# Moving an attention kernel's sums to VectorE, half of its k copies to ScalarE and its transposes later

## Chip, cores, metric

One core of a Trainium2 chip. The metric is device time in microseconds (us) of one execution; lower is better. Profiles are of one execution each; their spans are some 2 us shorter than the timed figure of the same execution. Runs of one kernel scatter: the kernel before took 337.5 to 350.8 us within one set of rounds. So comparisons rest on several runs of each kernel, taken in the same rounds on the same chip, and a run over 1.5% above the fastest of its kernel counts as slow and is left out.

## The reference, cut to what matters

```python
# q, k, v: (8 batches, 8 heads, 576 positions, 64), fp32
q_d, k_d, v_d = means of q, k, v over groups of 4 positions
out = repeat(softmax(q_d k_d^T / 8) v_d, 4)            # coarse attention
    + softmax(q k^T / 8 where |i - j| < 4) v           # local band attention
x = out as (4608 tokens, 512)
y = gelu(x @ w_in) @ w_out                             # w_in 512 x 2048, w_out 2048 x 512
```

The kernel computes in fp16 with fp32 sums. x is processed in 9 chunks of 512 tokens. **M1** is x @ w_in with the gelu (64 matmuls of 128x512 a chunk), **M2** is g @ w_out (64 more). The attention of batch b is woven into M2 of chunk b-1.

## The kernel before

```python
def m1(c):                       # a generator: each yield is one matmul
    ...
    for j in range(3 if c == 0 else 0, NJ):
        ps = mm()                # two PSUM tiles in turn
        for fc in range(4):
            nc.tensor.matmul(out=ps, lhsT=w_in_sb[:, fc, 128*j:128*j+128],
                             rhs=xT[:, fc, 512*c:512*c+512], start=(fc == 0), stop=(fc == 3))
            if fc == 3:
                nc.scalar.activation(out=g[:, j, :], in_=ps, func=ACTF.Gelu)
            yield

def cross_k():                   # regroup on VectorE, then turn by a DMA transpose
    for i in range(NP): regroup("kn", i)
    nc.sync.dma_start_transpose(out=kP..., in_=REG["kn"])
def cross_q(b): ...              # the same for q

def k_in(p):                     # k as the score matmuls want it, and its sums of four
    for hh in range(2):
        nc.vector.tensor_copy(out=kz[r, p, hh, :].rearrange("p (t r) -> p t r", r=6),
                              in_=kP[r, :, p, :].rearrange("p r t -> p t r"))
    ...                          # three VectorE adds
def q_sums(b, p): ...            # two adds on GpSimd
def v_down(b): ...               # five small operations on GpSimd

# chunk c, b = c + 1 (for 1 < b < 7; batch 7 is the last and loads no next one)
load6(b+1, "kn"); load6(b+1, "qn")
v_down(b)
for p in range(NP): k_in(p); q_sums(b, p)
k_lo()
run(load_v(b+1)); cross_k()
f1()                             # all of M1
attn(b, f2)                      # attention; f2(n) drops n matmuls of M2 between its parts
```

In `attn`, a pair p of heads goes through `scores` (matmuls, then exponentials on ScalarE), `mask` (VectorE times the band), `av` (matmuls, then the norm on VectorE) and `t_out` (transposes, then an add into xT). `cross_q(b + 1)` stood behind the first mask. A PSUM tile is a buffer that matmuls write their sums to; with two in turn, M1's next matmuls wait until ScalarE's gelu has read the older one. Names in the profile lines: `k_turned` and `qT` are k and q after their transposes, `kz` is k laid out for the score matmuls, `kdz` and `KL` hold k's sums of four, `q_t` and `qd` q's, `v_d` and `v_lm` v's; `sc` are scores, `e` exponentials, `sl` the scores against `KL`.

The softmax here doesn't subtract the row's maximum and nothing guards it: scores larger than these inputs give would overflow.

## Time and profile before

| | before |
|---|---|
| timed, us (first 3 runs) | 348.05 median, 344.29 to 350.76 |
| profiled span, us | 340.5 (of another execution, timed at 342.2) |
| TensorE busy | 325.6 us, 96% |
| stages of chunks 1 to 6, us (start of M1 to start of the next M1) | 37.8, 36.6, 35.2, 35.2, 34.4, 34.3 |

The stages come from the starts of the M1 blocks in the TensorE timeline. The prediction below shows the lines behind them. Beside those, the timeline of the queue that issues the transposes tells when each begins (start, length of the issue, line):

```profile
62.02 3.94 SPq L143 DMA_TRANSPOSE k_turned<-k_nat  x1
66.09 10.72 SPq L148 DMA_TRANSPOSE qT<-q_nat  x1
88.80 8.48 SPq L143 DMA_TRANSPOSE k_turned<-k_nat  x1
97.39 8.61 SPq L148 DMA_TRANSPOSE qT<-q_nat  x1
120.29 5.99 SPq L143 DMA_TRANSPOSE k_turned<-k_nat  x1
126.44 7.43 SPq L148 DMA_TRANSPOSE qT<-q_nat  x1
```

M1 of chunk 1 begins at 67.8 and needs the second batch's k and q some 15 us later; M1 of chunk 2 begins at 105.6. From batch 4 on (the third k and q above), q's transpose is issued 13 to 16 us ahead of the M1 of its stage.

### The profile page before, as it was taken

How to read it: one execution, taken by the hardware profiler on the slowest of the kernel's cores; microseconds unless marked ns; L12 is line 12 of the kernel's file. 1: busy time of each engine (PE TensorE's matmuls, PEld its weight loads, DVE VectorE, ACT ScalarE, POOL GpSimd, SP SyncE). 2: the span in 40 equal slices, each digit the busy share in tenths (PEclk: the TensorE clock that was granted, in tenths of full speed). 3: DMA queues.
4: the chain of work that ended last, by engine and by line, in shares of the span. 5: the costliest groups of instructions: out<-in, count | busy, mean ns of one | idle time of the engine just before them, and what ended most of it. 6: DMA issues, size and time to landing. Idle time of an engine off the chain costs nothing.

```text
span 340.5 us, 6382 instructions
## 1 busy us (share of the span) xinstructions
PE 325.6 (96%) x2586; PEld 178.6 (52%) x2586; DVE 210.4 (62%) x388; ACT 200.5 (59%) x368; POOL 145.9 (43%) x182
## 2 busy tenths in 40 slices
PE   7999999899799997999999999999999999999995
PEld 4665555544464455545654565446544654444444
DVE  7955945839977968695869686878695650000000
ACT  9675875467464675467646754675467646524610
POOL 8973393344961687393807780085560000000000
PEclk9999999999999999999999999999999999999999
DMA  6999999996699999989991999909950010011011
GB/s 80 166 193 204 202 171 201 163 167 75 68 128 156 194 121 172 185 128 164 154 129 58 128 119 178 126 3 130 192 88 0 33 64 31 2 62 63 0 54 71
DMA packets 99693, 39.34 MB, mean 116 GB/s; under 512 B 71632, under 2 KB 95184, under 8 KB 99664
## 3 DMA queue, kind: packets, MB, share of 16 engines
q0 software_dynamic: 66304, 22.42, 64.2%
q1 hardware_dynamic: 28320, 7.34, 22.3%
q10 hardware_dynamic: 5040, 9.18, 9.7%
q8 instruction: 20, 0.33, 0.4%
q14 instruction: 9, 0.07, 0.1%
HBM read 44.83 MB, written 9.44 MB: 159 GB/s over the span
## 4 chain that ended last, share of the span: by engine, by line
PE 75%; DVE 14%; DMA 6%; ACT 3%; issue 1%; POOL 1%; DVEq 0%
PE m_ps L233 32%; PE m_ps L257 28%; DMA k_turned<-k_nat 4%; PE sc L383 3%; DVE e L421 3%; DVE nall L458 3%; PE av L443 2%; DMA k_nat<-in_k_dram 2%; DVE kz L269 2%; PE tr_o L485 2%; DVE q_nat L135 2%; DVE k_nat L135 1%; PE m_ps L248 1%; DVE kdz L278 1%; PE av L435 1%
## 5 line engine op out<-in xcount | busy, mean ns | idle before, releaser
L257 PE MATMUL m_ps<-w_out_sb,gT 128*128 128x512 f16 x560 | 130.5, 379 | 0.0
L233 PE MATMUL m_ps<-xT,w_in_sb 128*128 128x512 f16 x564 | 125.5, 379 | 0.8 <-DVE xT L488 0.5
L236 ACT ACTIVATE gT<-m_ps 128x512 f16<-128x512 f32 x141 | 84.2, 597 | 38.8 <-PE m_ps L233 37.2
L233 PEld LDWEIGHTS <-w_in_sb 128*128 128x128 f16 x564 | 54.6, 98 | 66.4 <-issue 3.0
L257 PEld LDWEIGHTS <-gT 128*128 128x128 f16 x560 | 51.9, 98 | 54.3
L289 POOL TENSOR_TENSOR q_t<-qT 128x288 f32<-128x288 f16 x28 | 25.2, 898 | 63.1 <-DMA qT<-q_nat 62.9
L261 ACT COPY out_sb<-m_ps 128x512 f32<-128x512 f32 x35 | 20.6, 589 | 45.2 <-PE m_ps L257 45.2
L269 DVE COPY kz<-k_turned 64x576 f16<-64x576 f16 x48 | 36.2, 754 | 6.8 <-DMA k_turned<-k_nat 6.1
L421 DVE TENSOR_TENSOR e<-e,band 128x1152 f16<-128x1152 f16 x28 | 27.5, 981 | 20.6 <-ACT e L415 20.6
L488 DVE TENSOR_TENSOR xT<-tr_o,xd 128x576 f16<-128x576 f16 x28 | 21.2, 756 | 23.1 <-ACT xd L487 23.1
L252 DVE COPY out_sa<-m_ps 128x256 f32<-128x256 f32 x2 | 0.8, 424 | 55.1 <-PE m_ps L248 55.1
L458 DVE TENSOR_TENSOR nall<-av,rr 128x896 f16<-128x896 f32 x30 | 32.7, 1092 | 1.0
L113 POOL DMA_DIRECT2D v_win<-in_v_dram x30 | 27.0, 922 | 0.5 <-PE sc L383 0.5
L383 PE MATMUL sc<-qT,kz 128*128 128x114 f16 (+2 forms) x320 | 25.6, 216 | 0.0
L487 ACT COPY xd<-tr_o 128x144 f16<-128x144 f16 x28 | 7.7, 274 | 27.6 <-PE tr_o L485 24.8
L413 ACT ACTIVATE e<-sc 128x684 f16<-128x684 f32 x32 | 23.5, 736 | 0.0
L383 PEld LDWEIGHTS <-kz 128*128 128x128 f16 x320 | 21.5, 97 | 1.4
L278 DVE TENSOR_TENSOR kdz<-k_t 64x144 f16<-64x144 f32 x48 | 18.6, 387 | 1.4
L415 ACT ACTIVATE e<-sc 128x468 f16<-128x468 f32 x32 | 18.1, 566 | 0.7 <-PE sc L383 0.7
L443 PE MATMUL av<-v_win,e 128*128 128x65 f16 x300 | 14.1, 194 | 4.1 <-DVE e L421 4.1
L411 ACT ACTIVATE ed<-sc 128x288 f16<-128x288 f32 x32 | 13.0, 406 | 6.6 <-PE sc L383 6.5
L291 POOL TENSOR_TENSOR qd<-q_t 128x144 f16<-128x144 f32 x28 | 15.1, 539 | 2.2
(168 smaller groups left out, 385.2 us busy)
## 6 DMA issues: line engine op xcount, KB each, us to landing
out_dram<-out_sb ACTq DMA_DIRECT2D x35, 256.0 KB, 6.1
v_win<-in_v_dram POOLq DMA_DIRECT2D x40, 128.0 KB, 11.4
k_nat<-in_k_dram POOLq DMA_DIRECT2D x7, 576.0 KB, 13.8
q_nat<-in_q_dram POOLq DMA_DIRECT2D x7, 576.0 KB, 17.8
v_grp<-in_v_dram POOLq DMA_DIRECT2D x6, 512.0 KB, 8.1
w_in_sb<-in_moe_w_in_dram POOLq DMA_DIRECT2D x4, 512.0 KB, 9.2
w_out_sb<-in_moe_w_out_dram POOLq DMA_DIRECT2D x4, 512.0 KB, 19.1
v_lo<-in_v_dram POOLq DMA_DIRECT2D x6, 64.0 KB, 7.8
```

The lines of the kernel that those rows point to most:

```text
L113: nc.gpsimd.dma_start(out=L["vw"][:, j, :, 0:64], in_=v[b, :, W0[j]:W0[j] + 128, :].rearrange("h s d -> s h d"))
L233: nc.tensor.matmul(out=ps, lhsT=w_in_sb[:, fc, 128 * j:128 * j + 128], rhs=xT[:, fc, 512 * c:512 * c + 512], start=(fc == 0), stop=(fc == 3))
L236: nc.scalar.activation(out=g[:, j, :], in_=ps, func=ACTF.Gelu)
L257: nc.tensor.matmul(out=ps, lhsT=g[:, j, 128 * t:128 * t + 128], rhs=w_out_sb[:, j, :], start=(j == 0), stop=(j == NJ - 1))
L269: nc.vector.tensor_copy(out=kz[r, p, hh, :].rearrange("p (t r) -> p t r", r=6), in_=kP[r, :, p, :].rearrange("p r t -> p t r"))
L278: nc.vector.tensor_tensor(out=kdz[r, p, hh, :], in0=t2[r, :, 0], in1=t2[r, :, 1], op=ALU.add)
L289: nc.gpsimd.tensor_tensor(out=t2.rearrange("p g i -> p (g i)").rearrange("p (t u) -> p u t", u=3), in0=qp[:, :, 0, :], in1=qp[:, :, 1, :], ...
L383: nc.tensor.matmul(out=dst, lhsT=kz[:, p, hh, W0[j]:W0[j] + 128], rhs=q6(b)[:, :, p, Q0[j] // 6:(Q0[j] + QW[j]) // 6], start=(b > 0), stop ...
L413: nc.scalar.activation(out=e2[:, :, 0:EA], in_=sc2[:, :, 0:EA], func=ACTF.Exp, scale=0.125)
L421: nc.vector.tensor_tensor(out=e2, in0=e2, in1=band.unsqueeze(1).broadcast_to([128, 2, S]), op=ALU.mult)
L458: nc.vector.tensor_tensor(out=nall.rearrange("p j a c -> p a j c"), in0=av4[:, :, :, 0:64], in1=rr.unsqueeze(3).broadcast_to([128, 2, 7, 6 ...
L488: nc.vector.tensor_tensor(out=xT[:, p, S * b:S * b + S].rearrange("p (g r) -> p g r", r=4), in0=tr[:, 0:S].rearrange("p (g r) -> p g r", r=4),
```

## The change

Its intent, as I read it: GpSimd's sums hold up VectorE (a mask of 3.31 us beside one of them, where its peers take 0.75), so VectorE takes them and GpSimd only issues loads. To make room, ScalarE takes half of the kz copies, M1 gets a third PSUM tile to ride over them, and k's regroups move from the M1 half of a stage into the M2 half. M1 of chunk 1 is begun early to fill the hole at the end of batch 1's attention.

```diff
     def m1(c):
-        for j in range(3 if c == 0 else 0, NJ):
-            ps = mm()
+        first = 1 - turn[0]
+        if c:
+            turn[0] = first
+        if c == 1:
+            ...                        # three tiles: 9 matmuls (fc 0 to 2), then fc 3
+        for j in range(3 if c < 2 else 0, NJ):
+            if c == 0:
+                ps = mm()
+            elif j % 3 == (0 if c == 1 else 1):
+                ps = ppool.tile([128, 512], F32, tag="tr", name="m_ps")
+            else:
+                ps = bank(first if j % 3 == (2 if c == 1 else 0) else 1 - first)
     def k_in(p):
-        for hh in range(2):
+        for hh, cp in ((1, nc.scalar.copy), (0, nc.vector.tensor_copy)):
-            nc.vector.tensor_copy(out=kz..., in_=kP...)
+            cp(out=kz..., in_=kP...)
     def q_sums(b, p):
+        eng = nc.gpsimd if b == 1 else nc.vector
     def v_down(b):
-        eng = nc.gpsimd
+        eng = nc.vector
     def attn(b, fill):
         mask(0)
         if 1 < b < B - 1:
-            cross_q(b + 1)
+            for i in range(NP):
+                regroup("kn", i)
+            cross_k()
 ...                                    # per pair p:
             t_out(b, p)
+            ...                        # b == 1: k behind pairs 0 and 1, q by ScalarE behind 1 and 2
+            elif 1 < b < B - 1:
+                for i in ((0,), (1,), (2, 3), ())[p]:
+                    regroup("qn", i)
+            if b + 1 < B and p == 2:
+                cross_q(b + 1)
 # chunk c, b = c + 1
-            v_down(b)
+                run(load_v(b + 1))     # straight behind the q load
+            if b == 2:
+                f1(12)
             for p in range(NP):
                 k_in(p)
-                q_sums(b, p)
+                if p:
+                    q_sums(b, p - 1)
+                f1(12)
+            q_sums(b, NP - 1)
             k_lo()
-            if b + 1 < B:
-                run(load_v(b + 1))
-                cross_k()
+            v_down(b)
+        if b == 1:
+            g1 = m1(1)
+            f2 = filler(chain(m2(c), islice(g1, 9)))
```

(Cut: the counts of matmuls between the parts of `attn`, the order of batch 1's masks, the line that resumes `g1`, and that `cross_k` and `cross_q` lose their regroups, which are now called one by one.)

More of the change, by code (lines that the diff above doesn't have):

```diff
@@ L1 @@
+from itertools import chain, islice
 from contextlib import ExitStack
@@ L132, in reg, with regroup @@
         return REG[nm].rearrange("p (r h d) -> p r h d", r=6, h=H)[:, :, 2 * p:2 * p + 2, :]
-    def regroup(nm, p):
-        nc.vector.tensor_copy(
+    def regroup(nm, p, cp=None):
+        (cp or nc.vector.tensor_copy)(
             out=reg(nm, p),
@@ L140, in cross_k @@
     def cross_k():
-        for i in range(NP):
-            regroup("kn", i)
         nc.sync.dma_start_transpose(out=kP.rearrange("p r a t -> p (r a) t"), in_=REG["kn"])
     def cross_q(b):
-        for i in range(NP):
-            regroup("qn", i)
         nc.sync.dma_start_transpose(out=q6(b).rearrange("p r a t -> p (r a) t"), in_=REG["qn"])
@@ L229, in m1 @@
                         yield
-        for j in range(3 if c == 0 else 0, NJ):
-            ps = mm()
+        first = 1 - turn[0]
+        if c:
+            turn[0] = first
+        if c == 1:
+            t = ppool.tile([128, 1536], F32, tag="sc", name="m_ps")
+            part = [bank(first), t[:, 0:512], t[:, 512:1024]]
+            for fcs in ((0, 1, 2), (3,)):
+                for j in range(3):
+                    for fc in fcs:
+                        nc.tensor.matmul(out=part[j], lhsT=w_in_sb[:, fc, 128 * j:128 * j + 128],
+                                         rhs=xT[:, fc, 512:1024], start=(fc == 0), stop=(fc == 3))
+                        if fc == 3 and j == 2:
+                            for i in range(3):
+                                nc.scalar.activation(out=g[:, i, :], in_=part[i], func=ACTF.Gelu)
+                        yield
+        for j in range(3 if c < 2 else 0, NJ):
[5 more added lines that the diff above has]
+                ps = bank(first if j % 3 == (2 if c == 1 else 0) else 1 - first)
             for fc in range(4):
@@ L266, in k_in @@
     def k_in(p):
-        for hh in range(2):
+        for hh, cp in ((1, nc.scalar.copy), (0, nc.vector.tensor_copy)):
             r = slice(64 * hh, 64 * hh + 64)
-            nc.vector.tensor_copy(out=kz[r, p, hh, :].rearrange("p (t r) -> p t r", r=6),
-                                  in_=kP[r, :, p, :].rearrange("p r t -> p t r"))
+            cp(out=kz[r, p, hh, :].rearrange("p (t r) -> p t r", r=6),
+               in_=kP[r, :, p, :].rearrange("p r t -> p t r"))
         kp = kP[:, :, p, :].rearrange("p (u i) t -> p u i t", i=2)
@@ L288, in q_sums @@
         t2 = wpool.tile([128, Sd, 2], F32, tag="qt2", bufs=2, name="q_t2")
-        nc.gpsimd.tensor_tensor(out=t2.rearrange("p g i -> p (g i)").rearrange("p (t u) -> p u t", u=3),
+        eng = nc.gpsimd if b == 1 else nc.vector
+        eng.tensor_tensor(out=t2.rearrange("p g i -> p (g i)").rearrange("p (t u) -> p u t", u=3),
                                 in0=qp[:, :, 0, :], in1=qp[:, :, 1, :], op=ALU.add)
-        nc.gpsimd.tensor_tensor(out=qd[:, p, :], in0=t2[:, :, 0], in1=t2[:, :, 1], op=ALU.add)
+        eng.tensor_tensor(out=qd[:, p, :], in0=t2[:, :, 0], in1=t2[:, :, 1], op=ALU.add)
     def t_reg(nm, p, trf, sums):
@@ L500, in attn @@
     def attn(b, fill):
-        n = (6, 9, (5, 0, 0, 4), (5, 9, 9, 11), (10, 3)) if b == 1 else (6, 9, (0, 0, 0, 4), (9, 9, 9, 13))
+        n = (4, 8, (3, 0, 0, 2), (9, 9, 10, 12), (9, 2)) if b == 1 else (6, 9, (0, 0, 0, 4), (9, 9, 11, 11))
         fill(n[0])
@@ L520, in attn @@
                     fill(n[4][x - 1])
+                    mask(x)
                     if x == 1:
-                        mask(1)
                         v_down_pe(b)
@@ L527, in attn @@
                 mask(p + 1)
-            if b == 1 and p + 2 < NP:
-                mask(p + 2)
             if b == 1 and p == 1:
-                cross_k()
-            if b == 1 and p == 2:
-                cross_q(2)
+                mask(3)
             fill(n[3][p])
             t_out(b, p)
+            if b == 1 and p < 2:
+                regroup("kn", 2 * p)
+                regroup("kn", 2 * p + 1)
+                if p == 1:
+                    cross_k()
+            if b == 1 and p in (1, 2):
+                regroup("qn", 2 * p - 2, nc.scalar.copy)
+                regroup("qn", 2 * p - 1, nc.scalar.copy)
+            elif 1 < b < B - 1:
[3 more added lines that the diff above has]
+                cross_q(b + 1)
     def filler(g):
@@ L661 @@
         b = c + 1
-        f1 = filler(m1(c)) if c else f1_0
+        f1 = filler(g1 if c == 1 else m1(c)) if c else f1_0
         if b == 1:
@@ L695 @@
                 load6(b + 1, "qn")
-            v_down(b)
+                run(load_v(b + 1))
+            if b == 2:
+                f1(12)
             for p in range(NP):
                 k_in(p)
-                q_sums(b, p)
+                if p:
+                    q_sums(b, p - 1)
+                f1(12)
+            q_sums(b, NP - 1)
             k_lo()
-            if b + 1 < B:
-                run(load_v(b + 1))
-                cross_k()
+            v_down(b)
         f1()
         f2 = filler(m2(c))
+        if b == 1:
+            g1 = m1(1)
+            f2 = filler(chain(m2(c), islice(g1, 9)))
         if b < B:
```

## The prediction

> **What bounds the kernel now.** I read the page first. Its busy line says that TensorE (PE) is busy for 96% of the span, so the most that a change of order can win is TensorE's holes.
>
> ```profile
> PE 325.6 (96%) x2586; PEld 178.6 (52%) x2586; DVE 210.4 (62%) x388; ACT 200.5 (59%) x368; POOL 145.9 (43%) x182
> ```
>
> The holes are found by stage. One stage is M1 of a 512-token chunk (64 matmuls), then M2 of that chunk (64 matmuls) with the attention of the next batch woven in. I took the starts of the M1 blocks from the chain of work that ended last and asked for the table by windows (columns: window, length, then busy time and count of PE, PEld, DVE, ACT and POOL, granted clock, DMA share, GB/s).
>
> ```profile
> 44.40:66.00 21.60, 20.85 (x214) 12.45 (x211) 12.42 (x25) 12.68 (x25) 10.38 (x15) 1.00 1.62 182
> 66.00:105.78 39.78, 36.25 (x292) 19.59 (x291) 28.98 (x50) 22.21 (x42) 24.43 (x28) 1.00 1.09 115
> 105.78:142.35 36.57, 34.63 (x282) 19.00 (x280) 29.11 (x48) 21.82 (x41) 19.54 (x23) 1.00 1.43 163
> 142.35:177.51 35.16, 34.45 (x282) 19.05 (x280) 27.29 (x48) 21.82 (x41) 19.96 (x22) 1.00 1.41 154
> 177.51:212.67 35.16, 34.45 (x282) 19.06 (x280) 28.06 (x47) 21.82 (x41) 19.77 (x22) 1.00 1.17 118
> 212.67:247.10 34.43, 34.43 (x281) 18.94 (x280) 26.75 (x48) 21.82 (x41) 16.87 (x20) 1.00 1.03 113
> 247.10:281.37 34.27, 34.27 (x281) 19.02 (x280) 23.43 (x39) 21.82 (x41) 6.20 (x8) 1.00 0.19 45
> ```
>
> The last of these is a stage with PE busy throughout: 34.27 us is what the same PE work costs without holes. So chunks 2, 3, 4 and 5 lose 2.3, 0.9, 0.9 and 0.2 us against it, 4.3 us in all. Chunk 1 runs from 67.8 (PE timeline) to 105.6, 37.8 us, and loses 3.5. Before that, the PE timeline shows holes of 0.39, 0.36, 0.62 and 0.51 us from 57 to 69 us. The head (before 44 us) and the tail are not touched by the change. The ceiling of the gain is therefore about 9.5 us, 2.8% of the span, and only if everything fits.
>
> What makes the holes: the DVE and POOL timelines put an attention mask of 3.31 us for one instruction, whose peers take 0.75, over a 2.13 us sum on GpSimd, in chunk 2. The next matmul group waits for that mask.
>
> ```profile
> 127.03 3.31 DVE L421 TENSOR_TENSOR e<-e,band 128x1152 f16<-128x1152 f16 x1
> 127.59 2.13 POOL L349 TENSOR_TENSOR v_t<-v_grp 128x1024 f32<-128x1024 f16 x1
> ```
>
> In chunk 1 the cause is another: VectorE sat idle until the transposed k landed at 74.15, and then the sums of k were late for the scores.
>
> ```profile
> 74.15 1.32 DVE L269 COPY kz<-k_turned 64x576 f16<-64x576 f16 x2 [5.09 <-DMA k_turned<-k_nat]
> ```
>
> [...] the mask above (two SBUF inputs) ends just after the GpSimd sum, and k_in copies beside GpSimd's q sums run up to 1.96 us for two, against 1.32 without. [...] from 134 to 136 us GpSimd's load queue and the transpose queue each moved 832 packets. [...]
>
> **The change part by part.** (1) GpSimd loses its sums (from batch 2 on): q sums 0.8 + 0.54 us four times a stage, v sums some 6 us. [...] the 4.3 us of chunks 2 to 5 should be recovered, if nothing else appears.
>
> (2) VectorE takes them over. A q sum has the shape of k_t (128x288, 0.57 us) and kdz (0.31): 0.87 a pair, 3.5 a stage. The v sums are 1024, 512, 128, 64 and 520 elements long; at about 1 ns each and 0.1 to 0.25 us fixed (xT: 576 elements in 0.67) I make it 3.1 us. It gives up half the kz copies: 4 x 0.66 = 2.6 us. Net +4 us on some 26 uncontended (23.4 in the last full stage plus 8 regroups of 0.3): about 30 of 34.3. It fits, barely. ScalarE gets 4 x 0.75 = 3 us on 21.8: it fits, and three PSUM tiles let M1 ride over one copy (two gelus of 0.6 and a copy of 0.75 against 0.86 us of matmul a tile). M1 already runs at 13.93 us for 64 matmuls, M2 at 13.81, so the third tile alone gains nothing.
>
> (3) The M1 head start: 9 matmuls of chunk 1 fill the hole ahead of the last t_out. I followed the new order matmul by matmul with the durations of before. The k regroups now sit ahead of later norms, so of the 0.62 + 0.51 us about 0.6 are won.
>
> (4) The transposes move. k's is issued some 5 us into M2, long before use. But **q's is now issued after the third t_out**, behind its last regroups: what follows on PE is 20 matmuls (4.3 us), one AV (0.55) and one t_out (0.35), less the 1.7 us until xT and two regroups are done, so 3.5 us before the next M1. Before it was issued about 6 us into M2, or 15 in chunk 1. And VectorE, which runs in order, now has the q sums ahead of k's pairs 2 and 3: it waits for q there. From the first q sum to the mask of pair 0 it has 4 x 0.87 + 2 x 1.85 + KL 0.6 + v 3.1 + mask 0.67 = 11.5 us. The first AV wants that mask 19 us into the stage (13.93 for M1, 5.06 for M2's start to the AV's second half in chunk 5: 226.60 to 231.66). So q must land by 7.5 us into M1, **11 us after issue**. How long does it take? In the view of one line's DMA times:
>
> ```profile
> DMA to landing us min/median/max: 15.3/15.7/24.4
> DMA to landing us min/median/max: 11.3/13.0/21.3
> ```
>
> The first is q's, which was queued behind k's transpose; the second k's. The case nearest to the new q (nothing ahead of it, one load of 576 KB issued beside it) is k at 62.0 and 156.5 us: 12.1 and 11.3. So q lands 0.3 to 1.1 us too late, and the k regroups behind the mask delay the next norm by another 0.3. I take 0.8 us for each of chunks 2 to 5: +3.2. Chunk 6 has no loads beside it: 0.
>
> (5) Chunk 1. k's transpose is issued when it was (62 to 63), in the same company, and lands at 74 to 75; M1's gelus wait behind the ScalarE copy for some 1.9 us. q's follows and landed at 81.5 in the kernel before. From there the 11.5 us chain puts the mask at 93, where the AV ran at 89.5 before: +4, less the 0.6 us of the later norm wait: +3.4.
>
> Sum: -0.6 - 4.3 + 3.2 + 3.4 = +1.7 us, on 348.05. The two positive terms are the shaky ones. The change looks tuned for q to be there earlier, and I cannot see how GpSimd's new timing shifts the transfers, so I shade it to **348.5 us**.
>
> **The rivals.** (a) Everything fits: q lands within 11 us because most of it is moved before the load beside it has got going (k at 160 to 162 us moved 1593 of its 2360 packets in 2 us). Then chunks 2 to 5 go to 34.3 and chunk 1 breaks even or gains 1 to 2: 341 to 343. For it: the spread of single-packet rates; against it: no k transpose took under 11.3. (b) The transfers collide: GpSimd, now free, issues the v loads straight behind q's load, so the q transpose shares with both; before, they came after the q sums. Then q takes 13 to 16 us, and chunks 2 to 5 stall 2 to 5 us each: 356 to 368. For it: k took 12.5, 13.6, 16.9 and 21.3 where v loads ran. Against it: v is behind the q load in its queue. (c) VectorE becomes the bound without any DMA: the v sums are slower than I think, and the AV waits for them. With 30 of 34.3 us used it has room for some 3 us a stage; above that each microsecond costs six.
>
> **Range and chances.** Ceiling of the gain 9.5 us: 338.5 is the low end of what is possible and I put the low at 339. The high is rival (b) at its mild end, 359. Faster by over 2% needs 7 us, nearly all of the ceiling: 0.24. Slower by over 2% needs the q wait at over 2 us a stage: 0.24. Between: 0.52. The runs of before spread from 344.3 to 350.8, which adds 2 us each way.
>
> **What would show it.** Right for (1): no mask over 1 us in VectorE's timeline, no GpSimd sums after 50 us. Right for (4): VectorE's waits show a q sum waiting for the q transpose in chunks 2 to 5, and the q transpose lands 8 us or more into M1; the AV, or its weight load, waits for VectorE. If this wait is missing and the stages are 34.3 us, rival (a) holds. Right for (5): M1's matmuls of chunk 1 show a hole of 1 to 2 us behind a gelu, and the first AV after it comes at 93 or later. Right for (c) instead: VectorE has no idle time in the M1s and the AV still waits. The prediction is wrong if q's landing is off by more than 2 us in either direction, since it is multiplied by four.

## The result

The changed kernel ran at 357.01 us median (354.59 to 358.58, 4 runs) against 346.3 (344.29 to 350.76, 4 runs) for the kernel before. The ratio is **1.032** (95% interval 1.022 to 1.043). Ratios here are the mean time of one kernel's fast runs over that of the other's of the same rounds, so they are not quite the ratio of the medians.

The two profiled spans are 340.5 and 352.9 us, 12.4 apart. In the table by windows of the changed kernel, cut at the M1 starts as before (window, length, then busy time and count of PE, PEld, DVE, ACT, POOL, clock, DMA share, GB/s):

```profile
67.90:113.95 46.05, 37.01 (x281) 19.55 (x279) 26.65 (x56) 25.50 (x45) 9.31 (x12) 0.93 1.19 120
113.95:152.27 38.32, 35.56 (x281) 19.01 (x280) 26.05 (x56) 25.89 (x45) 7.80 (x10) 1.00 1.17 127
152.27:187.60 35.33, 34.81 (x282) 19.02 (x281) 26.24 (x56) 25.86 (x45) 7.82 (x10) 1.00 1.00 133
258.22:293.58 35.36, 34.80 (x281) 19.00 (x280) 24.30 (x48) 25.90 (x45) 0.00 (x0) 1.00 0.12 38
```

Chunk 1 costs 8.2 us more than before (46.0 against 37.8), chunk 2 1.7, chunks 3 to 6 0.2, 0.2, 0.9 and 1.1. With 0.1 ahead of chunk 1 this is the whole 12.4. (At 67.9, four of chunk 1's 64 M1 matmuls, 0.9 us, are already done; before, none.) Chunks 3 to 6 are all alike, at 35.3: even chunk 6, which has no load beside it and only the last 1.9 us of q's transpose, and which stood at 34.3 before.

What was sought did come. The masks on VectorE took 748 to 759 ns, against up to 3312 before:

```profile
L441 DVE TENSOR_TENSOR e<-e,band x28: 748/749/759, 47.0 to 287.4; 128x1152 f16<-128x1152 f16 x28
```

What it cost, in the chain of work that ended last (start, length, what), in chunk 1:

```profile
65.95 19.57 DMA qT<-q_nat
85.61 0.55 DVE q_t L309
86.50 0.57 DVE kz L288
...
95.20 0.70 DVE v_lm L374
95.90 0.68 DVE e L441
96.62 0.73 PE av L463 x10
97.36 3.72 PE m_ps L276 x9
```

q's transpose took 19.6 us to land. From there the chain runs through VectorE for 10.3 us until the mask begins, and only then comes the first AV. The nine matmuls behind it took 3.72 us; the same nine elsewhere take 1.94. The granted clock from 97.4 to 101.0 was 0.52, after TensorE had been busy for only 5.5 of the 12.9 us from 84.5 on, with one hole of 3.46 us. So this stall was followed by a second loss: after the waiting, 1.8 us of slower matmuls. That the stall lowered the clock is my reading of the order; the trace does not show what sets it.

The waits of the changed kernel name both this and something else (who, for whom: total, times, longest):

```profile
DVE q_t L309 <- DMA qT<-q_nat: 26.5, 5, 8.2
PE sl L386 <- DVE KL L363: 3.5, 1, 3.5
PE m_ps L252 <- ACT gT L255: 3.0, 6, 1.5
PE sc L409 <- DVE qd L311: 1.9, 1, 1.9
```

And in chunk 3 the chain runs through ScalarE from 152.5 to 163.8, for 11.3 of M1's 15.0 us:

```profile
152.47 0.59 ACT out_sb L280
...
153.47 1.19 ACT kz L288
154.66 0.03 issue
154.69 1.57 ACT gT L255 x3
156.26 0.02 issue
156.28 1.17 ACT kz L288
```

The kz copy takes ScalarE 1.19 us. The one line's view has both engines on the same shape:

```profile
L288 ACT COPY kz<-k_turned x24: 1169/1194/1216, 74.0 to 267.9; 64x576 f16<-64x576 f16 x24
L288 DVE COPY kz<-k_turned x24: 631/644/652, 74.0 to 265.3; 64x576 f16<-64x576 f16 x24
```

Three gelus and a copy are then 2.81 us from copy to copy, and the 12 matmuls beside them 2.59 (12 of 0.216). M1 waits for ScalarE.

### The profile page after: what moved, and what is told of

It is laid out like the page before. It is cut to its first block, busy times and chain, and to the rows that moved or that the text cites.

```text
span 352.9 us, 6344 instructions
## 1 busy us (share of the span) xinstructions
PE 330.9 (94%) x2586; PEld 179.6 (51%) x2586; DVE 202.4 (57%) x438; ACT 227.5 (64%) x396; POOL 77.3 (22%) x104
## 4 chain that ended last, share of the span: by engine, by line
PE 57%; ACT 14%; DVE 13%; DMA 11%; POOL 1%; issue 1%; ACTq 0%; DVEq 0%; POOLq 0%; SPq 0%
PE m_ps L276 28%; PE m_ps L252 12%; DMA qT<-q_nat 10%; ACT gT L255 6%; ACT kz L288 5%; PE sc L403 4%; PE av L463 2%; PE tr_o L505 2%; DVE kdz L301 1%; DVE q_t L309 1%; DMA k_turned<-k_nat 1%; PE m_ps L267 1%; DVE kz L326 1%; PE sc L409 1%; DVE nall L478 1%
## 5 line engine op out<-in xcount | busy, mean ns | idle before, releaser
L276 PE MATMUL m_ps<-w_out_sb,gT 128*128 128x512 f16 x560 | 132.3, 383 | 0.0
L252 PEld LDWEIGHTS <-w_in_sb 128*128 128x128 f16 x552 | 53.3, 97 | 71.7 <-issue 11.2
L255 ACT ACTIVATE gT<-m_ps 128x512 f16<-128x512 f32 x138 | 77.3, 598 | 16.7 <-PE m_ps L252 14.4
L280 ACT COPY out_sb<-m_ps 128x512 f32<-128x512 f32 x35 | 20.6, 588 | 39.9 <-PE m_ps L276 39.9
L508 DVE TENSOR_TENSOR xT<-tr_o,xd 128x576 f16<-128x576 f16 x28 | 21.2, 758 | 27.8 <-ACT xd L507 27.8
L288 ACT COPY kz<-k_turned 64x576 f16<-64x576 f16 x24 | 28.6, 1192 | 4.1 <-ACT out_sb L280 2.0
L441 DVE TENSOR_TENSOR e<-e,band 128x1152 f16<-128x1152 f16 x28 | 21.0, 751 | 15.1 <-ACT e L435 15.1
L114 POOL DMA_DIRECT2D v_win<-in_v_dram x30 | 28.0, 946 | 3.8 <-DMA k_nat<-in_k_dram 3.7
L309 DVE TENSOR_TENSOR q_t<-qT 128x288 f32<-128x288 f16 x24 | 13.2, 551 | 26.7 <-DMA qT<-q_nat 26.5
L129 POOL DMA_DIRECT2D k_nat<-in_k_dram x10 | 7.6, 760 | 85.9 <-DVE rr L477 83.7
L129 POOL DMA_DIRECT2D q_nat<-in_q_dram x10 | 7.8, 784 | 48.5 <-DVE rr L477 43.5
L288 DVE COPY kz<-k_turned 64x576 f16<-64x576 f16 x24 | 15.4, 643 | 4.9 <-DMA k_turned<-k_nat 4.8
## 6 DMA issues: line engine op xcount, KB each, us to landing
k_nat<-in_k_dram POOLq DMA_DIRECT2D x7, 576.0 KB, 10.8
v_lo<-in_v_dram POOLq DMA_DIRECT2D x6, 64.0 KB, 12.9
```

Of the source, the lines that this page charges most:

```text
L114: nc.gpsimd.dma_start(out=L["vw"][:, j, :, 0:64], in_=v[b, :, W0[j]:W0[j] + 128, :].rearrange("h s d -> s h d"))
L252: nc.tensor.matmul(out=ps, lhsT=w_in_sb[:, fc, 128 * j:128 * j + 128], rhs=xT[:, fc, 512 * c:512 * c + 512], start=(fc == 0), stop=(fc == 3))
L276: nc.tensor.matmul(out=ps, lhsT=g[:, j, 128 * t:128 * t + 128], rhs=w_out_sb[:, j, :], start=(j == 0), stop=(j == NJ - 1))
L280: nc.scalar.copy(out=osb, in_=ps)
L288: cp(out=kz[r, p, hh, :].rearrange("p (t r) -> p t r", r=6), in_=kP[r, :, p, :].rearrange("p r t -> p t r"))
L441: nc.vector.tensor_tensor(out=e2, in0=e2, in1=band.unsqueeze(1).broadcast_to([128, 2, S]), op=ALU.mult)
```

## The experiments

Two theories. **Q**: VectorE runs in order, and its q sums stand in front of half of k's work and all of v's; the late q transpose delays everything behind it. (In chunk 1 of the changed kernel its third kz copy began at 86.41, behind a q sum that had waited for q until 85.61; k had landed at 74.00.) **S**: ScalarE's kz copies make M1 wait. Beside them, the **collision** of the v loads with the transposes. All kernels gave correct results. "Changed" is the changed kernel; the stage lengths and landing times are from one profiled run each, the stages from M1 start to M1 start; chunk 1 is counted from the first M1 matmul behind the last t_out (in the kernels with the head start, 4 of the 64 are done by then, 0.9 us).

| run | edit | ratio to before | chunk 1 | chunk 2 | chunks 3 to 6 | k, q of batch 2: issue to landing |
|---|---|---|---|---|---|---|
| before | | 1 | 37.8 | 36.6 | 35.2, 35.2, 34.4, 34.3 | 12.1, 15.3 |
| changed | | 1.032 (1.022 to 1.043) | 46.0 | 38.3 | 35.3 each | 11.7, 19.6 |
| e1 | kz on VectorE | 1.030 (1.023 to 1.037) | 49.1 | 35.4 | 35.2, 34.8, 35.7, 34.2 | 13.5, 21.2 |
| e2 | q sums last | 1.006 (1.003 to 1.010) | 40.2 | 35.3 | 35.3 each | 12.0, 20.4 |
| e3 | ScalarE reads in rows | 1.087 (1.079 to 1.095) | 47.3 | 39.0 | 39.0 each | 13.1, 20.6 |
| e4 | all v loads late | 1.122 (1.112 to 1.132) | 41.9 | 49.1 | 44.4, 47.8, 39.2, 35.3 | 12.8, 16.6 |
| e5 | e1 + e2 | 0.994 (0.991 to 0.996) | 40.9 | 34.2 | 34.2 each | 11.7, 19.8 |
| e6 | e5, batch 2 turned earlier | 1.006 (1.004 to 1.009) | 44.3 | 34.2 | 34.2 each | 21.0, 27.6 |
| e7 | two PSUM tiles | 1.079 (1.068 to 1.090) | 45.7 | 39.4 | 38.3 each | 11.5, 20.0 |
| e8 | q sums on GpSimd | 1.009 (1.006 to 1.012) | 39.6 | 35.3 | 35.3 each | 13.9, 19.5 |
| e9 | e5, batch 3's v late | 1.024 (1.013 to 1.035) | 43.0 | 40.5 | 34.2 each | 13.6, 15.6 |
| e10 | e9 without head start | 1.022 (1.013 to 1.030) | 42.3 | 40.7 | 34.2 each | 11.9, 16.9 |
| e11 | before, v sums on VectorE | 0.993 (0.990 to 0.997) | | | | |
| e12 | e5, v sums first | 0.994 (0.992 to 0.997) | 39.9 | 34.2 | 34.2 each | 14.2, 20.4 |

What follows rests on the stages.

### e1: both kz copies on VectorE

```diff
-        for hh, cp in ((1, nc.scalar.copy), (0, nc.vector.tensor_copy)):
+        for hh, cp in ((1, nc.vector.tensor_copy), (0, nc.vector.tensor_copy)):
```

> The changed kernel with both kz copies back on VectorE. Theory S (ScalarE's kz copies of 1.19 us make M1 wait for ScalarE): the stages of chunks 3 to 6 fall from 35.3 to 34.3 us, M1's hole behind a gelu in chunk 1 (1.5 us) goes, the first AV of chunk 1 stays late for q; in all 4 to 6 us less than the changed kernel, ratio to before about 1.017. Rival Q (only the late q transpose matters): stages 3 to 6 stay at 35.3 or grow by VectorE's extra 2.6 us, ratio 1.03 or more.

The total hardly moved, but the stages did. Chunk 6, where q lands 5.4 us after issue, fell to 34.2: M1 is no longer held by ScalarE. Chunks 3 to 5, where q takes 10.2 to 11.0, stayed between 34.8 and 35.7, because the longer chain on VectorE is now the one that is late. Chunk 1 grew by 3: q landed 1.9 us later than in the changed kernel, and two more copies stand in the chain behind it. Neither theory alone describes this: with S mended, Q takes its place.

### e2: q sums behind k_in and the v sums

```diff
                 k_in(p)
-                if p:
-                    q_sums(b, p - 1)
                 f1(12)
-            q_sums(b, NP - 1)
-            k_lo()
             v_down(b)
+            for p in range(NP):
+                q_sums(b, p)
+            k_lo()
```

> The changed kernel with VectorE's q sums moved behind all of k_in and the v sums, so that only the q sums and KL wait for q. Theory Q (VectorE, in order, stands behind the q transpose): after q lands VectorE needs 5 us to the first mask in place of 10.8; chunk 1 shrinks by 5 to 7 us (its AV at about 91 and no half clock behind it), chunk 2 by 1 to 2; ratio about 1.012. Rival S (ScalarE alone): no change, 1.032.

Theory Q holds for chunks 1 and 2: 5.8 and 3.0 us less, though q landed no earlier in chunk 1 (20.4 us after issue). The order of instructions on one engine was worth 2.6% of the whole. Chunks 3 to 6 stayed at 35.3, as S says. One part of the expectation was a miss: the half clock still came, at 0.53 from 88.6 to 92.2, where the nine matmuls took 3.58 us (2.10 in the same view of e7); the longest hole just before was 2.36 us.

```profile
87.67 0.22 PE L409 MATMUL sc<-qd,kdz 128*128 128x144 f16 x1 [2.36 <-DVE qd L311]
88.33 3.58 PE L276 MATMUL m_ps<-w_out_sb,gT 128*128 128x512 f16 x9
```

### e3: the same copy, walked in the other order

```diff
+            if hh == 1:
+                cp(out=kz[r, p, hh, :].rearrange("p (t r) -> p r t", r=6), in_=kP[r, :, p, :])
+                continue
```

> The changed kernel; ScalarE's kz copy walks its input in rows (reads one after the other, writes 12 bytes apart) in place of reading 768 bytes apart; same values. If the far-apart reads make it slow: 0.6 to 0.7 us in place of 1.19, and the stages of chunks 3 to 6 fall to 34.3 to 34.6, 3 to 5 us in all. If ScalarE is slow on any 16-bit data in SBUF: stays at 1.19 and the time stays at 1.032.

My guess about the reads was a miss: with reads one after the other and writes 12 bytes apart the copy took longer still. The same view of one line:

```profile
L289 ACT COPY kz<-k_turned x24: 2097/2118/2132, 75.9 to 284.2; 64x576 f16<-64x576 f16 x24
```

The run is the best evidence for S nevertheless, as a dose: a copy costs 0.92 us more (2.12 against 1.19), a stage has four, and chunks 3 to 6 grew by 3.7 (39.0 against 35.3). ScalarE's time in M1 went into the span one for one here: 4 x 0.92 = 3.7.

### e4: no v load beside the q transposes

```diff
-                run(load_v(b + 1))
...
+            if b + 1 < B:
+                nc.gpsimd.tensor_copy(out=gd, in_=qd[:, NP - 1, 0:2])
+                run(load_v(b + 1))
```

> The changed kernel; GpSimd issues the v loads only once the last q sum is there (a tiny GpSimd copy reads it first), so no v load is in flight beside the q transpose. Collision theory: the q transposes of chunk 1 and 2, 19.6 and 15.2 us to landing, take 13 to 15 and 9 to 11; 4 to 6 us less in all, ratio about 1.017. Rival: v stands behind the q load in its queue anyway, q lands when it did, ratio 1.03.

The collision is real in chunk 1: q landed 16.6 us after issue in place of 19.6, and chunk 1 shrank by 4.1. The packets show it too: from 80 to 82 us the load queue and the transpose queue moved 487 and 490 in the changed kernel, 18 and 851 here. But the v loads then ran into the next k transpose, which took 22.0, 19.4 and 21.0 us in the next stages in place of 9 to 10, and everything behind it slid. The delay was moved, not removed, and it grew.

### e5: both finds mended

The edits of e1 and e2 together.

> The changed kernel with both finds mended: kz copies on VectorE and q sums behind k_in and v sums. If the two causes are separate and add up: stages of chunks 3 to 6 at 34.2 us (35.3 in the run with q sums last), ratio 1.006 - 5.5/343 = 0.990. If VectorE with all the copies becomes the bound: the first AV of each stage waits for the mask by more than 0.5 us, stages at 34.7 or more, ratio above 0.997.

Each of chunks 2 to 6 takes 34.2 us, as TensorE's work alone would have it:

```profile
178.00:212.15 34.15, 34.15 (x281) 19.04 (x280) 29.03 (x60) 21.94 (x41) 7.89 (x10) 1.00 1.04 137
```

So Q and S are separate and add up in these chunks: from 35.3 to 34.2 by the copies, from 38.3 to 35.3 in chunk 2 by the order. VectorE, with all the copies and all the sums, is busy for 29.0 us of the stage and holds nothing up. This kernel beats the changed one, and the kernel before by 0.65%; how much depends on which runs of the latter count (over all runs of the same set of rounds the medians are 341.2 and 344.4, 0.9%; the means of the fast ones 341.3 and 342.3, 0.3%). What is left is chunk 1.

### e6: batch 2's transposes issued earlier

```diff
             av(b, p)
+            if b == 1 and p == 0:
+                for i in range(NP):
+                    regroup("kn", i)
+                cross_k()
...                                        # q behind the first two t_outs, by VectorE
```

> As the run before, and batch 2's k and q transposed earlier: k regrouped after the first AV of batch 1, q after its first two t_outs, so k's transpose is issued near 57.6 in place of 62.3 and q's near 62.3 in place of 66. If the rest of chunk 1's loss is the late transposes: k lands before 71 and M1's hole of 1.9 us behind a gelu goes, q lands near 82 in place of 86.6; 3 to 4 us less than the run before, ratio about 0.980. If the DMA engines are simply full there and q lands when it did: 1.9 us at most, 0.985.

This backfired. k's transpose was issued at 58.5 in place of 63.1 and landed at 79.5 in place of 74.8:

```profile
k_turned<-k_nat SPq DMA_TRANSPOSE x1, 21.0
```

In the DMA view by 2 us, batch 2's own v loads still ran until some 64 (2421 packets from 58 to 60), and k's transpose moved no packet before 60. From 70 to 80 its queue and the load queue, which had gone on to the next k, q and v, moved about as many packets each, 125 to 300 in 2 us. q then came behind k, at 92. The earlier issue was no gain here: the transpose met loads that were still running and landed 4.7 us later.

### e7: two PSUM tiles in M1

```diff
-        if c:
+        if c == 1:
             turn[0] = first
...
-            if c == 0:
+            if c != 1:
                 ps = mm()
```

> The changed kernel with two PSUM tiles in M1 from chunk 2 on, as before. If the third tile carries M1 over ScalarE's copies: each copy of 1.19 us now stops TensorE, stages of chunks 3 to 6 grow from 35.3 by 0.5 to 2 us; ratio 1.04. If M1 is bound by ScalarE's sum of work only: unchanged, 1.032.

Chunks 3 to 6 went from 35.3 to 38.3. TensorE's timeline shows its stop behind the copies (in brackets: idle before, for whom):

```profile
156.27 2.75 PE L252 MATMUL m_ps<-xT,w_in_sb 128*128 128x512 f16 x12 [1.16 <-ACT gT L255]
159.80 2.75 PE L252 MATMUL m_ps<-xT,w_in_sb 128*128 128x512 f16 x12 [0.78 <-ACT gT L255]
163.34 2.75 PE L252 MATMUL m_ps<-xT,w_in_sb 128*128 128x512 f16 x12 [0.79 <-ACT gT L255]
```

With the copies in ScalarE's order the third tile saves 3.0 us a stage, more than the 2 I had allowed.

### e8: q sums back on GpSimd

```diff
-        eng = nc.gpsimd if b == 1 else nc.vector
+        eng = nc.gpsimd
```

> The changed kernel with the q sums alone back on GpSimd (v sums stay on VectorE). Theory Q: VectorE no longer stands behind q; chunk 1 shrinks by 4 to 6 us, chunk 2 by 1 to 2, steady stages stay near 35.3, bound by ScalarE; ratio about 1.01. If VectorE's own load were the trouble, the gain would be the 3.5 us a stage in every stage: ratio under 1.0. If neither: 1.032.

As Q has it: chunk 1 6.5 us shorter, chunk 2 3.0, chunks 3 to 6 not at all. It gives about what e2 gives: what counts is that VectorE no longer stands behind q. That VectorE's own load is not the trouble cannot be read here, since ScalarE holds chunks 3 to 6 anyway; e5, with more on VectorE and stages of 34.2, shows it.

### e9 and e10: chunk 1, v held back once; and the head start

```diff
+                if b > 2:
                     run(load_v(b + 1))
...
                 q_sums(b, p)
+                if b == 2 and p == 0:
+                    nc.gpsimd.tensor_copy(out=gd, in_=qd[:, 0, 0:2])
+                    run(load_v(b + 1))
```

> The mended kernel (kz copies on VectorE, q sums last) with one more edit: GpSimd issues batch 3's v loads only after the first q sum of batch 2, so that they are not in flight beside batch 2's transposes. Collision theory: q lands near 82.6 as in the run where all v loads wait, in place of 86.6; the score hole of 5.2 us in chunk 1 goes to about 1, chunk 1 from 40.9 to 36 to 37 us, later stages stay at 34.16; ratio 0.9935 - 4/344 = 0.982. If q lands when it did: 0.993. If the moved loads run into batch 3's k transpose, chunk 2's M1 waits for it: above 0.99.

> The kernel of the run before without the head start of M1 of chunk 1 (its 9 matmuls after the attention, as before the change). If the head start fills the hole ahead of the last t_out of batch 1: 1.1 us more, ratio 0.003 higher. If chunk 1 is still set by the landing of q, which the head start doesn't move: no difference.

A miss, with the third case that I had named. q did land earlier, at 82.8 in place of 86.6. But the first score of chunk 1 came at 89.7, no earlier than in e5 (88.6):

```profile
89.66 0.28 PE L410 MATMUL sc<-qd,kdz 128*128 128x144 f16 x1 [6.90 <-DVE qd L312]
```

k had landed at 76.1, and k_in with both copies takes VectorE 9.5 us, the v sums 3.1: the chain from k's landing ends at 88.7, whatever q does. In e5, too, it ended at 87.7, after q. And the held loads ran into the next k (20.3 us to landing) and q (20.9), so chunk 2 lost 6 us. e10 takes the head start away and costs nothing that these runs can resolve (ratios 1.022 and 1.024, each with an interval of about 1% either way): while chunk 1 waits for its k and q, it does not matter whether nine matmuls are done in advance.

### e11: one part alone on the kernel before

```diff
     def v_down(b):
-        eng = nc.gpsimd
+        eng = nc.vector
```

> The kernel before with one part of the change alone: the v sums on VectorE, the q sums left on GpSimd. [...] no mask over 1 us, holes of chunks 2 to 4 gone, 3 to 4 us less, ratio about 0.990. If VectorE's 3.1 us more a stage eat it up: 1.0.

The fast runs are 0.7% below those of before. The longest of the 28 masks took 978 ns (3312 before), so the hold-up of VectorE went with GpSimd's v sums. This one line brings about as much as e5, perhaps more: one quick run of the kernel before, 337.5, left only 7 of its 27 runs counted as fast in that set of rounds, and over all runs the medians are 338.6 and 343.5, 1.4% apart.

### e12: v sums in the idle time before k lands

```diff
+            v_down(b)
             if b == 2:
                 f1(12)
...
-            v_down(b)
```

> The mended kernel with VectorE's v sums moved ahead of k_in, so that in chunk 1 they fill the 4.9 us in which VectorE stands idle before k lands. In the mended kernel the k chain (10 us of k_in from 74.9, then 3.1 of v sums) ends at 87.7, one microsecond after q landed at 86.6. If that chain sets the first score of chunk 1: the score starts at 87.5 in place of 88.6, the mask follows from q sums and KL 1.1 earlier, chunk 1 is 1 to 2 us shorter, later stages stay at 34.16; ratio 0.9935 - 0.004 = 0.989. If q alone sets it, 0.993.

In the profile the first score came at 87.6, as expected, and now waits for q, which landed at 86.6; chunk 1 took 39.9. In the timed runs no difference to e5 is resolved (0.994 and 0.994).

## Why the prediction came out as it did

The range of 339 to 359 held the 357.0, but the middle of it did not: I had put the likeliest change at about nothing, and slower by over 2% at 0.24. That the range held it is in part luck. Its upper end stood for transfers that collide in each of chunks 2 to 5; what came was a longer chunk 1 (8.2 of the 12.4 us), ScalarE in chunks 3 to 6 (2.4), and chunk 2 (1.7). By the steps:

- **GpSimd's hold-up of VectorE (part 1)** was right in what matters. The masks are 0.75 us throughout, and e11 shows the worth of the v sums by themselves. The trace of before shows that the long masks and GpSimd's sums coincide, not how the one delays the other: the three masks over 1 us (3.31, 2.53, 2.53) each ran beside a GpSimd sum of 2.13 us; two began after it, but the one shown began 0.56 us ahead of it.
- **VectorE's load (part 2)** was right in its parts: the v sums took 3.15 us (I had 3.1; 1.23, 0.70, 0.28, 0.22 and 0.70 for the 1024, 512, 128, 64 and 520 elements), a q sum 0.9 (0.87). The sum of 30 us was too high: 26.2 in chunk 3. The 23.4 that I built on was no uncontended figure; its stage held kz copies that ran up to 1.96 us for two beside GpSimd's q sums (1.32 without).
- "ScalarE gets 4 x 0.75 = 3 us on 21.8: it fits" is **the step that failed**. I took a VectorE duration for ScalarE; the copy took 1.19. And I looked at the sum over the stage, where it does fit (25.9 of 35.3), not at M1, where three gelus and a copy are 2.81 us against 2.59 of matmuls. (With the 0.75, and the 1.57 that the three gelus take, it would have fitted there too.) This is the 35.3 of chunks 3 to 6. It costs 1.1 us a stage: more than the 0.9 that part 1 could win in chunks 3 and 4, the 0.2 in chunk 5 and the nothing in chunk 6. "The third tile alone gains nothing" was true of M1 without copies; with them e7 puts it at 3.0 us.
- **The q transposes (part 4)**: the mechanism was right, the place was off. q's landing does stop VectorE (five waits, 26.5 us in all). But in chunks 3 to 5 it took 10.1 to 10.8 us, not 11.3 to 12.1, just within the 11 I had allowed, and the mask of the first AV there waited for ScalarE's exponentials. The 0.8 us for each of these is not there. In chunk 2 it took 15.2 and cost 3.0 us over the others. Why 15.2, and as much in e3 and e7 (15.3, 16.3), where e1, e2, e5, e8 and e12 show 10.5 to 10.8, is left open. Little of the loads' data moved beside it: from 114 to 120 us the load queue moved 14 to 42 packets in 2 us, and the transpose itself went slowly, 360 to 698, where it reached 1416 in e1. In chunk 6, with no load beside it, q's transpose took 5.2 to 5.4 us; the longest, 27.6, was that of batch 2 in e6, behind k's and beside the next loads.
- **Chunk 1 (part 5)** was mis-sized: +3.4 predicted, +8.2 measured. k's landing (74.0) and the hole behind a gelu (1.5 us, I had 1.9) were right. q landed at 85.6, not 81.5: more than the 2 us that I had named as the sign of being wrong, and the collision that I had as rival (b) and set aside because v stands behind the q load in its queue. Where the v loads wait (e4, e9, e10), q of batch 2 takes 15.6 to 16.9 us; in the eight other runs with the changed order of loads and the same issue times it takes 19.5 to 21.2. And I had no term for the clock: 1.8 us on nine matmuls (3.72 against 1.94, at a clock of 0.52). The runs give no length of a hole that is safe: the matmuls were slow behind holes of 3.46 us (changed), 2.36 (e2, nine in 3.58 us) and 2.63 (e4, M1 of chunk 1: 32 in 8.75 us, 7.51 in e2), but not behind one of 2.56 (e7, nine in 2.10 us).
- **The head start (part 3)**: in the profile, 0.9 us of M1 is done where the stage of chunk 1 begins, 0.1 us later than before, so the 0.6 was about right there. It then vanishes in the wait for q. e10 shows no loss without it, but cannot resolve 0.6 us.

The rivals as a whole: (b) held in chunk 1 only; (c) is refuted by e5, where VectorE has still more to do and TensorE waits for nothing in chunks 2 to 6; and (a) describes chunks 3 to 6 as far as q goes, but ScalarE kept them from 34.3. The sum came out wrong by 11 us (+1.7 against 12.4 between the profiled spans) because two terms were missing, ScalarE's own time for the copy (1.19 us) and the lower clock in chunk 1 (0.52), and q in chunk 1 was 4 us late. The copy's time could not be read off: before, ScalarE copies kz only from PSUM, in 633 ns. But a warning stood in that profile, three small ScalarE copies with steps in SBUF, up to 765 ns for at most 120 elements, where 144 elements from PSUM take 278:

```profile
L564 ACT COPY turn<-Iw x3: 594/756/765, 6.1 to 6.7; 128x120 f16<-128x120 f16 x1, 128x114 f16<-128x114 f16 x1, 128x108 f16<-128x108 f16 x1
```

## What to carry to other kernels

Before work is moved to another engine, find that engine's own time for that access (here 1.19 us on ScalarE, 0.64 on VectorE), and compare it with the time of the stretch it falls in, not with its share of a whole stage. On an engine that runs in order, as VectorE did here, put what waits for a late transfer behind everything that does not: here that alone was worth 2.6%. And ask of every transfer issued earlier or later what it meets on the way; three of these twelve runs (e4, e6, e9) moved a load or a transpose off one wait and lost more at the next.
